# One step of a rational function's residual goes from VectorE to an adding DMA, with a new table of due times and another home for the ring of streamed weights

## Chip, cores, metric

The kernel runs on one core of one Trainium2 chip. The metric is the device time in microseconds of one execution. In what follows PE is TensorE, DVE is VectorE, ACT is ScalarE, POOL is GpSimd and SP is SyncE.

## What is computed

Three stages follow each other. Attention with a packed middle: `p` attends to `k`, `v`, and `q` attends to the result, for 8 batches, 8 heads, 576 positions and 32 packed rows. Then two feed-forward layers over the 4608 tokens of width 512, the first with a rational function, the second with h - tanh(h):

```
def _moe_ref(x, w_in, w_out, a, b):
    h = x @ w_in                      # 4608 x 512 @ 512 x 2048
    P = a[0] + a[1]*h + a[2]*h**2 + a[3]*h**3
    Q = 1.0 + abs(b[0])*abs(h) + abs(b[1])*h**2
    g = P / (Q + 1e-06)
    return g @ w_out                  # 2048 x 512
...
def _moe2_ref(x, w_in, w_out):
    h = x @ w_in
    return (h - tanh(h)) @ w_out
```

The weights arrive as float64 and are unpacked on the chip.

## The kernel before

Every product of the two layers is made from two reduced-precision parts, a high and a low one, so that each factor is split and three matmuls make one.

**Stage one** does attention and the first layer together. The tokens lie in 10 blocks (`XW`: 384, 512, 512, 512, 384, and the same again), and the 2048 hidden columns in 8 pairs of 128. A group g is one block with one pair: 80 groups, 48 of them with 2 x 512 = 1024 elements a partition and 32 with 768. For each group PE makes h (`l1`, line 643, two PSUM buffers), ACT and DVE make the polynomial P in tile `t` (lines 666, 681, 685), ACT makes |h| and a factor in `u` and `r` (670, 674), POOL or DVE multiplies them to the denominator in `m` (line 678, `front_q`), ACT turns it into a reciprocal `r` through Ln and Exp (690, 691), and `back` makes g in two parts for the second product (`l2`, line 656, with the high part 16 matmuls, with the low part 8):

- step 0 (698): the high part, gh = (t + a0) * r, rounded
- step 1 (700): m = (m + C0) * gh
- step 2 (704): m = (t + a0) - m, the residual
- step 3 (707): the low part, gl = m * r

The four are called b0 to b3 below; all four run on DVE. There are three `t`, two `m` and two `r`, with one more `m` and `r` in the middle of the stage, and one `gh` and one `gl` with one more each in the middle (`TEMPS`, `EXTRA`).

**The start** of stage one unpacks the weights: two `raw` tiles take turns, each filled by two transfers of 512 KB, shifted on DVE (342), scaled on ACT (350), joined on DVE (355), rounded on ACT (1215) and for the second weight split on DVE or POOL (1219).

**Stage two** (from about 780 us) is the second layer: tokens 0 to 511 with plain products (`l3`, line 770, and `l4`, lines 800 to 802), while combinations of the weights are prepared and stored to DRAM (833, 841, 850), then four blocks of 1024 tokens with seven products in place of eight, whose weights are streamed through a ring of four tiles (`ring_w`, used by line 977).

**The order** on every engine is set while the kernel is built, by the planner `Plan`: a list scheduler that knows a cost for each piece of work, picks what can start soonest on an engine, and among pieces that start within `SLACK` of that takes the one with the earliest due time. The due times come from the table `DUE`. Each engine then runs its list strictly in order, and waits on semaphores. What the costs say is the planner's; how long work takes is in the trace.

Of the kernel before, what the change touches and what calls it, by code (L numbers as in the profile page):

```python
# [7 lines left out]
F32 = mybir.dt.float32  # L8
# [8 lines left out]
LN_SHIFT = 63  # L17
LN2 = 0.6931471805599453


DUE = {"a_fq": 0.98, "a_b3": -15.108, "a_sl": -2.257, "a_sn": -4.221, "a_ss": -4.584, "a_xl": -7.444, "a_w4": -9.16, "a_w3": 15.573, "a_w2": -20.328, "G0": 4.368, "G1": 38.031, "A2": 4.694, "P_W": -6.643, "P_F": -18.924, "P_R": 2.448, "P_B": -19.51, "P_2": 3.012, "P_3": 12.129, "P_E": 10.733, "P_4": 17.691, "D_Y": -1.827, "b0": 22.093, "b1": -3.811, "b2": 2.98, "b3": -16.754, "l2h": 32.124, "l2l": 0.87, "f2": -30.567, "f3": -24.228, "fu": 3.235, "ft": 10.645, "fq": -31.176, "gH": -22.408, "gL": -35.399, "mx": -26.764, "ex": -60.969, "z": -8.638, "et": -7.472, "ta": 16.855, "av": -10.074, "y": 7.135, "bt": -42.785, "bd": -27.214, "si": -58.27, "sx": 25.69, "ss": 14.777, "se": -46.899, "sz": 13.095, "sn": 9.267, "so": 55.715, "sh": -7.194, "sl": -14.895, "w1": 20.251, "w2": -5.992, "w3": 17.226, "wh": -2.934, "wl": 18.386, "x": 7.951, "u2": 1.457, "u3": 13.153, "u4": 2.566, "u5": -25.368, "uu0": -1.378, "uu1": -1.334, "r0": -24.578, "dA": 37.158, "wd": -30.552, "d": 12.111}

SLACK = {"ALT": 0, "DVE": 7.5, "PE": 525.8, "ACT": 0, "POOL": 0, "SP": 734.4}

# [149 lines left out]
def packed_attention_moe_kernel(  # L174
# [81 lines left out]
    def pool_of(stack, name, bufs=1, **kw):  # L256
        return stack.enter_context(tc.tile_pool(name=name, bufs=bufs, reuse_waits="tile", **kw))
# [5 lines left out]

    tmp_p = pool_of(last, "tmp", side="right")

# [467 lines left out]
    oacc = {}  # L733
    yx = yt = stg = tw = None

# [6 lines left out]
    def x_load(b, k):  # L742
        t = yx.tile([128, 512], F32, tag="xr", name="xr", bufs=2)
        sp.dma_start(out=t, in_=x2d[:, k, NBLK * b:NBLK * b + NBLK])
        xr_t[b, k] = t
# [333 lines left out]
    def c_dve(n):  # L1079
        return 1.04 * n + 70  # L1080
# [156 lines left out]
    dma(("c",), 128 * 24, const_loads, due=-8)  # L1237
    add(("cabs",), "ACT", 100, lambda: act.activation(out=cabs, in_=cob, func=AF.Abs), [("c",)], -1)
    for b in range(B):
# [86 lines left out]


    add(("open t",), None, 0, close_start, [], 0, behind=[("bd", 0)])
    for g in range(total):
# [37 lines left out]
    def open_x():  # L1367
        nonlocal yx
        right.close()
        yx = pool_of(last, "yx", side="right")  # L1370
        x_buf(0)

    def open_y():
        nonlocal yt, stg, tw
        sx.close()
        stg = pool_of(ctx, "stg")
        ex = pool_of(ctx, "ex")
        yt = pool_of(ctx, "yt")
        tw = pool_of(ctx, "tw")
# [3 lines left out]
    sides = [("sl", NB - 1), ("g", B - 1, NP - 1), ("bd", 2 * B - 1), ("g", B - 1, NP - 2)]  # L1383
    add(("open x",), None, 0, open_x, sides, 0)
    add(("open y",), None, 0, open_y, [], 0,
# [11 lines left out]
    add(("open x", 1), None, 0, lambda: x_buf(1), [x for y in raw_user[-RAW:] for x in y], 0, behind=raw_next(("open x", 1)))  # L1397
    add(("open x", 2), None, 0, lambda: (x_buf(2), open_ring()), [("open x", 1), ("open x",)], 0)
    for b in range(3):
        for k in range(4):  # L1400
            e = d + (-12, 4, 20)[b] + 2 * k + O("x")
            n = 4 * b + k
            free = [("xl", *divmod(n - 2, 4))] if n >= 2 else []
            dma(("xr", b, k), 512 * 512, lambda b=b, k=k: x_load(b, k), [("open x",)] + reach(NBLK * b, NBLK) + free, e - 2 - 20 * (b > 0))
# [55 lines left out]
    for n, (kind, j) in enumerate(order):  # L1460
# [30 lines left out]
    for s in range(NS):  # L1491
# [82 lines left out]
        for n, i in enumerate(TWO):  # L1574
            for c in range(2):
                users = [("m4", s, i, f) for f in range(4 * c, 4 * c + 4)]
                have = [{1: ("pb", 4, j, 0), 2: ("pb", 4, j, 1), 3: ("pb", 4, j, 1)}.get(i, ("pd", 4, j)) for j in range(4 * c, 4 * c + 4)] if s == 0 else []
                if s == 0 and n < 2:
                    have += [("open x", 2), ("l3", n + 1, NF - 1)]
                stream(("wl4", s, n, c), 128 * 8192, lambda s=s, n=n, c=c: load_w4(s, n, c), have,  # L1580
# [33 lines left out]
        end = lambda i: ("m4", s, i, NJ2 - 1)  # L1614
        tmp_free = lambda x: [(x, s, NJ2 - 1)] if s else []
        for y in range(2):
# [70 lines left out]
```

## Time and profile before

| | |
|---|---|
| three timed runs | 1537.21, 1539.22, 1540.37 us, median 1539.22 |
| the profiled execution | 1536.59 us, its span 1534.7 us, so 1.9 us lie around the span |
| busy share of the span | PE 95%, DVE 85%, ACT 57%, POOL 9% |
| mean granted clock of PE | 0.985 |

The share of busy time is a mean over stages that differ: stage one and stage two are to be read apart. PE's matmuls are pipelined and the ends of their records are modelled, so a short wait can lie inside a busy PE.

### The profile page before, as it was taken

What the parts mean: (1) busy time and instruction counts of PE and PEld (TensorE: products, weight loads), DVE (VectorE), ACT (ScalarE), POOL (GpSimd) and SP (SyncE); (2) the same over time, 40 slices, a digit from 0 to 9 for tenths busy, and PEclk for the clock granted to TensorE, in tenths of its full rate; (3) what the DMA queues carried; (4) which work ended last, traced back from release to release, by engine and by line L of the source; (5) the groups of instructions that cost most, each with busy time, mean ns of one, the idle gap of its engine ahead of it and who ended that gap; (6) DMA issues with size and microseconds to landing.
All of it is one profiled execution on the core that took longest, in us unless ns stands there. A gap on an engine that the chain in (4) does not pass through costs nothing.

```text
span 1534.7 us, 21747 instructions
## 1 busy us (share of the span) xinstructions
PE 1462.3 (95%) x8448; PEld 1194.2 (78%) x8448; DVE 1307.3 (85%) x1690; ACT 878.3 (57%) x1216; POOL 135.2 (9%) x82
## 2 busy tenths in 40 slices
PE   5768999999999999999989999999999999999999
PEld 2657787878888878788877887777788878887787
DVE  5988999999999999999987885797789577957685
ACT  4776676677677767677766542453345333633353
POOL 0100011112111101222012110000000000000000
PEclk8888999999999999999999999999999999999999
DMA  7783314221332303132134696776656655665553
GB/s 255 269 267 129 125 56 143 86 103 59 136 119 76 132 31 132 60 131 83 42 109 187 193 279 250 280 290 221 246 204 241 222 182 206 231 218 192 205 192 137
DMA packets 74998, 257.86 MB, mean 168 GB/s; under 512 B 7184, under 2 KB 25744, under 8 KB 60048
## 3 DMA queue, kind: packets, MB, share of 16 engines
q1 hardware_dynamic: 74896, 256.47, 48.0%
q8 instruction: 67, 1.10, 0.3%
q14 instruction: 35, 0.29, 0.1%
HBM read 204.02 MB, written 52.43 MB: 167 GB/s over the span
## 4 chain that ended last, share of the span: by engine, by line
PE 68%; DVE 21%; ACT 5%; issue 3%; DMA 2%; POOL 1%; SPq 0%; DVEq 0%; ACTq 0%; POOLq 0%
PE acc L977 17%; PE acc L656 16%; PE h L977 12%; PE h L643 9%; PE h L770 9%; DVE yl L1020 2%; PE h L509 2%; DVE t L685 1%; DMA raw<-in_w_dram 1%; DVE gh L698 1%; DVE t L681 1%; DVE gl L707 1%; DVE m L704 1%; DVE m L700 1%; DVE slot L1012 1%
## 5 line engine op out<-in xcount | busy, mean ns | idle before, releaser
L643 PE MATMUL h<-ah,slot 128*128 128x320 f32 (+3 forms) x1024 | 215.8, 305 | 1.8 <-DVE slot L521 1.8
L656 PE MATMUL acc<-gh,slot 128*128 128x512 f32 (+1 forms) x800 | 177.6, 375 | 11.7 <-DVE slot L1219 11.3
L656 PEld LDWEIGHTS acc<-gh,slot 128*128 128x128 f32 x800 | 149.5, 195 | 36.0 <-DVE slot L1219 12.8
L643 PEld LDWEIGHTS h<-ah,slot 128*128 128x128 f32 x1024 | 171.4, 193 | 3.2 <-DVE slot L521 2.0
L656 PE MATMUL acc<-raw,slot 128*128 128x512 f32 (+1 forms) x720 | 164.6, 379 | 0.0
L643 PE MATMUL h<-al,slot 128*128 128x192 f32 (+3 forms) x512 | 151.4, 309 | 8.2 <-DVE t L685 4.1
L656 PEld LDWEIGHTS acc<-raw,slot 128*128 128x128 f32 x720 | 130.2, 188 | 31.9 <-issue 10.5
L1016 ACT ACTIVATE yh<-slot 128x512 fp32r<-128x512 f32 x140 | 87.0, 630 | 72.5 <-PE acc L977 30.6
L678 POOL TENSOR_TENSOR m<-u,r 128x1024 f32<-128x1024 f32 (+1 forms) x33 | 72.5, 2198 | 480.0 <-ACT r L674 372.7
L643 PEld LDWEIGHTS h<-al,slot 128*128 128x128 f32 x512 | 98.3, 192 | 18.0 <-DVE slot L521 2.9
L670 ACT ACTIVATE u<-h 128x1024 f32<-128x1024 f32 (+1 forms) x80 | 74.5, 931 | 60.7 <-PE h L643 60.4
L1020 DVE TENSOR_TENSOR yl<-slot,yh 128x512 fp32r<-128x512 f32 x140 | 95.5, 693 | 15.6 <-ACT yh L1016 14.8
L681 DVE TENSOR_TENSOR t<-t,h 128x1024 f32<-128x1024 f32 (+1 forms) x80 | 88.3, 1106 | 9.2 <-ACT t L666 8.9
L666 ACT ACTIVATE t<-h,coa 128x1024 f32<-128x1024 f32 (+1 forms) x80 | 89.3, 1119 | 10.9 <-PE h L643 6.5
L685 DVE SCALAR_TENSOR_TENSOR t<-t,coa,h 128x1024 f32<-128x1024 f32 (+1 forms) x80 | 93.3, 1166 | 1.9 <-ACT u L670 1.2
L656 PE MATMUL acc<-gl,slot 128*128 128x384 f32 (+1 forms) x400 | 92.3, 372 | 2.1 <-DVE gl L707 2.0
L690 ACT ACTIVATE r<-m,lnb 128x1024 f32<-128x1024 f32 (+1 forms) x60 | 63.6, 1060 | 53.7 <-POOL m L678 36.6
L770 PE MATMUL h<-xh,slot 128*128 128x512 f32 x256 | 83.9, 399 | 8.0 <-DVE t L779 6.4
L656 PEld LDWEIGHTS acc<-gl,slot 128*128 128x128 f32 x400 | 70.7, 188 | 20.3 <-issue 7.2
L1016 ACT ACTIVATE yh<-ex 128x512 fp32r<-128x512 f32 x84 | 52.6, 631 | 50.6 <-PE acc L977 25.5
L977 PE MATMUL acc<-yh,raw 128*128 128x512 f32 x256 | 78.9, 389 | 0.0
L999 ACT ACTIVATE t<-slot 128x512 f32<-128x512 f32 x45 | 28.5, 633 | 85.8 <-DVE slot L992 48.8
(196 smaller groups left out, 3237.4 us busy)
## 6 DMA issues: line engine op xcount, KB each, us to landing
raw<-in_w_dram SPq DMA_DIRECT2D x64, 512.0 KB, 4.5
w<-w1d SPq DMA_DIRECT2D x28, 1024.0 KB, 4.8
raw<-w4d SPq DMA_DIRECT2D x28, 1024.0 KB, 4.8
xh<-w4d SPq DMA_DIRECT2D x14, 1024.0 KB, 4.8
xl<-w4d SPq DMA_DIRECT2D x14, 1024.0 KB, 5.3
xh<-w3d SPq DMA_DIRECT2D x12, 1024.0 KB, 5.1
raw<-w3d SPq DMA_DIRECT2D x12, 1024.0 KB, 5.0
k<-in_kT_dram SPq DMA_DIRECT2D x16, 576.0 KB, 4.0
```

What stands on the lines that cost most here:

```text
L643: pe.matmul(out=ps[:, f, t], lhsT=x, rhs=y, start=(i == 0), stop=(i == len(seq) - 1))
L656: pe.matmul(out=acc_t[n][m][:, 0:XW[n]], lhsT=w2_slot[2 * p + f][:, o:o + 128], rhs=x[:, f, :], start=(p == 0 and part == 512 and f == 0), ...
L666: act.activation(out=t_t[g], in_=hv(g), func=AF.Identity, scale=a3, bias=a2)
L670: act.activation(out=u_t[g], in_=hv(g), func=AF.Abs)
L678: by.tensor_tensor(out=q_m[g], in0=u_t.pop(g), in1=r_t[g], op=ALU.mult)
L681: dve.tensor_tensor(out=t_t[g], in0=t_t[g], in1=hv(g), op=ALU.mult)
L685: dve.scalar_tensor_tensor(out=t, in0=t, scalar=a1, in1=hv(g), op0=ALU.add, op1=ALU.mult)
L690: act.activation(out=r, in_=q_m[g], func=AF.Ln, scale=2.0 ** -LN_SHIFT, bias=lnb[:, 0:1])
L770: pe.matmul(out=hy(b, f), lhsT=a, rhs=w, start=(j == 0), stop=(j == len(seq) - 1))
L977: pe.matmul(out=to, lhsT=a, rhs=b, start=(first and n == 0 and i in (1, 6, 7, 5)), stop=(last and n == len(seq) - 1), skip_group_check=True,)
L1016: act.activation(out=yh_t[s, i, f], in_=g_of(GSRC[i], f), func=AF.Copy)
L1020: by.tensor_tensor(out=yl_t[s, i, f], in0=g_of(GSRC[i], f), in1=yh_t[s, i, f].bitcast(F32), op=ALU.subtract)
```

## The change

Step 2 of `back` becomes a DMA that POOL issues: it adds the tile t onto the tile m. For that the sign of m is turned (Ln gets a negative scale, step 1 a negative C0, the absolute coefficients are negated by one more ACT instruction), and a0 goes into step 3, which is now a scalar_tensor_tensor on DVE only. The planner counts the DMA as 1100 ns of POOL and 4000 ns until it has landed.

The tables `DUE` and `SLACK` are replaced as a whole. The ring of streamed weights consists of the two `raw` tiles and two tiles `rg` of its own; before, its second half was the pair of x tiles. The x tiles are loaded through `made` and `rg`, and the small temporaries `tmp` open only after the last `l3`.

```
     def recip(g):
         r = r_t[g]
-        act.activation(out=r, in_=q_m[g], func=AF.Ln, scale=2.0 ** -LN_SHIFT, bias=lnb[:, 0:1])
+        act.activation(out=r, in_=q_m[g], func=AF.Ln, scale=-(2.0 ** -LN_SHIFT), bias=lnb[:, 0:1])
...
         if step == 1:
             dve.scalar_tensor_tensor(
-                out=u, in0=u, scalar=C0, in1=gh_t[g].bitcast(F32), op0=ALU.add, op1=ALU.mult
+                out=u, in0=u, scalar=-C0, in1=gh_t[g].bitcast(F32), op0=ALU.add, op1=ALU.mult
             )
         if step == 2:
-            dve.scalar_tensor_tensor(out=u, in0=t, scalar=a0, in1=u, op0=ALU.add, op1=ALU.subtract)
+            pool.dma_start(out=u, in_=t, accum_op=ALU.add)
         if step == 3:
             gl_t[g] = tmp(g, "gl")
-            by.tensor_tensor(out=gl_t[g], in0=u, in1=r, op=ALU.mult)
+            dve.scalar_tensor_tensor(out=gl_t[g], in0=u, scalar=a0, in1=r, op0=ALU.add, op1=ALU.mult)
...
+    LAND = 4000
...
-        add(("b2", g), "DVE", c_dve(HW) + 60, lambda g=g: back(g, 2), [("b1", g)], g + P_B + O("b2"), port=True)
-        add(("b3", g), ("POOL", "DVE"), (c_pool(HW), c_dve(HW)), lambda by, g=g: back(g, 3, by), [("b2", g)] + temp_old["gl", g], g + P_B + O("b3"), port=True)
+        add(("b2", g), "POOL", 1100, lambda g=g: back(g, 2), [("b1", g)], g + P_B + O("b2"), late=LAND, port=False)
+        add(("b3", g), "DVE", c_dve(HW) + 60, lambda g=g: back(g, 3), [("b2", g)] + temp_old["gl", g], g + P_B + O("b3"), port=True)
...
     def open_ring():
-        for b in (1, 2):
-            ring_w.extend(x.rearrange("p k t -> p (k t)") for x in x_bufs[b])
+        ring_w.extend(x.rearrange("p k t -> p (k t)") for x in x_bufs[1])
+        ring_w.extend(rg.tile([128, 2048], F32R, tag=f"rg{i}", name=f"rg{i}") for i in range(2))
...
-SLACK = {"ALT": 0, "DVE": 7.5, "PE": 525.8, "ACT": 0, "POOL": 0, "SP": 734.4}
+SLACK = {"ALT": 0, "DVE": 9.8, "PE": 104.4, "ACT": 0.0, "POOL": 2003.4, "SP": 0.0}
```

Line numbers of the changed kernel are 12 higher in `back` and around it: 678 becomes 690, 681 becomes 693, 685 becomes 697, 698 becomes 710, 700 becomes 712, the DMA is line 716, step 3 is line 719, and 1219 becomes 1237.

The first place is DVE in the middle of stage one, around two groups of 1024 elements (the seventh block). Before:

```order
L698 SCALAR_TENSOR_TENSOR raw<-t_229,coa,r_233 128x1024
L700 SCALAR_TENSOR_TENSOR m_235<-m_235,raw 128x1024
L681 TENSOR_TENSOR t_230<-t_230,h 128x1024
L521 TENSOR_TENSOR slot_86<-h,slot_86 128x512
L685 SCALAR_TENSOR_TENSOR t_230<-t_230,coa,h 128x1024
L521 TENSOR_TENSOR slot_87<-h,slot_87 128x512
L704 SCALAR_TENSOR_TENSOR m_235<-t_229,coa,m_235 128x1024
L707 TENSOR_TENSOR raw<-m_235,r_233 128x1024
L698 SCALAR_TENSOR_TENSOR gh_237<-t_230,coa,r_234 128x1024
L700 SCALAR_TENSOR_TENSOR m_236<-m_236,gh_237 128x1024
L704 SCALAR_TENSOR_TENSOR m_236<-t_230,coa,m_236 128x1024
```

The same place of the changed kernel (712 is step 1, 719 is step 3; `raw` is the additional low or high part):

```order
L712 SCALAR_TENSOR_TENSOR m_237<-m_237,raw 128x1024
L533 TENSOR_TENSOR slot_89<-h,slot_89 128x512
L710 SCALAR_TENSOR_TENSOR gh_239<-t_232,coa,r_236 128x1024
L712 SCALAR_TENSOR_TENSOR m_238<-m_238,gh_239 128x1024
L719 SCALAR_TENSOR_TENSOR raw<-m_237,coa,r_235 128x1024
L693 TENSOR_TENSOR t_233<-t_233,h 128x1024
L693 TENSOR_TENSOR t_231<-t_231,h 128x1024
L697 SCALAR_TENSOR_TENSOR t_233<-t_233,coa,h 128x1024
L719 SCALAR_TENSOR_TENSOR gl_240<-m_238,coa,r_236 128x1024
```

Step 2 is gone from DVE, and between step 1 and step 3 of one group there now stand three instructions for the first group (m_237) and four for the second (m_238).

The second place is DVE at the start, around the second unpacked tile of the first group. Before:

```order
L698 SCALAR_TENSOR_TENSOR gh_237<-t_229,coa,r_233 128x768
L521 TENSOR_TENSOR slot_87<-h,slot_87 128x512
L700 SCALAR_TENSOR_TENSOR m_235<-m_235,gh_237 128x768
L1219 TENSOR_TENSOR slot_68<-raw,slot_68 128x512
L704 SCALAR_TENSOR_TENSOR m_235<-t_229,coa,m_235 128x768
L681 TENSOR_TENSOR t_230<-t_230,h 128x768
L685 SCALAR_TENSOR_TENSOR t_230<-t_230,coa,h 128x768
L681 TENSOR_TENSOR t_231<-t_231,h 128x768
L707 TENSOR_TENSOR gl_238<-m_235,r_233 128x768
```

And in the changed kernel:

```order
L712 SCALAR_TENSOR_TENSOR m_237<-m_237,gh_239 128x768
L354 TENSOR_SCALAR raw<-raw 128x1024
L367 SCALAR_TENSOR_TENSOR raw<-raw 128x1024
L533 TENSOR_TENSOR slot_87<-h,slot_87 128x512
L1237 TENSOR_TENSOR slot_68<-raw,slot_68 128x512
L1237 TENSOR_TENSOR slot_69<-raw,slot_69 128x512
L354 TENSOR_SCALAR raw<-raw 128x1024
L693 TENSOR_TENSOR t_232<-t_232,h 128x768
L719 SCALAR_TENSOR_TENSOR gl_240<-m_237,coa,r_235 128x768
```

The unpacking of the next weights now stands between step 1 and step 3 of the first group.

The third place is POOL in the second half of stage one, where blocks of 768 give way to blocks of 1024. Before it had only the products for the denominator:

```order
L678 TENSOR_TENSOR m_236<-u_232,r_234 128x768
L678 TENSOR_TENSOR raw<-u_232,raw 128x768
L678 TENSOR_TENSOR m_236<-u_232,r_234 128x1024
L678 TENSOR_TENSOR raw<-u_232,raw 128x1024
L678 TENSOR_TENSOR m_235<-u_232,r_233 128x1024
```

In the changed kernel it issues the adding DMAs between them:

```order
L690 TENSOR_TENSOR m_237<-u_234,r_235 128x768
L716 DMA m_237<-t_231 128x768
L716 DMA m_238<-t_232 128x768
L716 DMA raw<-t_233 128x768
L716 DMA m_237<-t_231 128x1024
L716 DMA m_238<-t_232 128x1024
L690 TENSOR_TENSOR raw<-u_234,raw 128x1024
```

POOL has 80 DMAs to issue, 37 products (47 before) and one split of line 1237 (16 before). DVE has 80 step-2 instructions fewer, 10 products and 15 splits more.

## Rows read from the trace of the kernel before

**Rows 1.** The page's first part: span, busy time, share of the span, instructions.

```profile
span 1534.7 us, 21747 instructions
PE 1462.3 (95%) x8448; PEld 1194.2 (78%) x8448; DVE 1307.3 (85%) x1690; ACT 878.3 (57%) x1216; POOL 135.2 (9%) x82
```

**Rows 2.** Busy time by stretch: length, PE, PEld, DVE, ACT, POOL, clock, DMA share, GB/s.

```profile
0.00:57.00 57.00, 34.45 (x340) 23.58 (x341) 37.39 (x53) 33.60 (x51) 5.84 (x9) 0.85 0.77 262
57.00:153.00 96.00, 71.12 (x650) 58.17 (x649) 84.62 (x110) 63.52 (x97) 4.22 (x2) 0.89 0.61 210
153.00:767.00 614.00, 607.67 (x4220) 507.20 (x4219) 596.00 (x613) 435.88 (x516) 96.23 (x44) 1.00 0.27 95
767.00:844.00 77.00, 70.11 (x324) 59.66 (x323) 62.00 (x75) 48.86 (x70) 14.69 (x11) 0.96 0.41 147
844.00:1535.00 691.00, 678.90 (x2921) 545.58 (x2919) 527.31 (x842) 296.46 (x485) 14.21 (x17) 1.00 0.64 222
```

**Rows 3.** PE's longest wait, 153 to 767 us: sum, times, longest.

```profile
PE h L643 <- DVE t L685: 2.0, 4, 1.0
```

**Rows 4.** Chain of work from 153 to 767 us: shares by line, one long piece.

```profile
by line: PE acc L656 35.5%; PE h L643 21.0%; issue 3.8%; PE h L509 3.7%; DVE gh L698 3.2%; DVE t L685 3.2%; DVE t L681 2.7%; DVE m L700 2.4%; DVE m L704 2.3%; DVE gl L707 2.3%; DVE slot L521 1.4%; POOL m L678 1.2%; ACT slot L517 1.1%; PE h 
277.62 7.30 PE acc L656 x32
```

**Rows 5.** Chain of work from 57 to 136 us: shares by line, two pieces.

```profile
by line: DMA raw<-in_w_dram 14.7%; issue 9.7%; PE acc L656 6.3%; DVE slot L1219 5.5%; DVE gl L707 4.6%; DVE raw L355 4.5%; DVE slot L521 3.9%; DVE t L685 3.7%; DVE m L704 3.7%; ACT r L690 3.5%; DVE m L678 3.4%; DVE mx L440 3.4%; ACT t L666 
...
51.24 6.20 DMA raw<-in_w_dram
74.16 1.22 DVE raw L355
```

**Rows 6.** PE's longest waits, 767 to 844 and 844 to 1535 us.

```profile
PE h L770 <- DVE t L779: 6.4, 1, 6.4
...
PE h L977 <- DVE yl L1020: 3.4, 5, 2.0
```

**Rows 7.** DVE's groups by form: busy us, mean ns of one, idle before.

```profile
L704 DVE SCALAR_TENSOR_TENSOR m<-t,coa,m 128x1024 f32<-128x1024 f32 x34 | 44.9, 1320 | 0.2
...
L704 DVE SCALAR_TENSOR_TENSOR m<-t,coa,m 128x768 f32<-128x768 f32 x26 | 26.3, 1012 | 0.3
L698 DVE SCALAR_TENSOR_TENSOR gh<-t,coa,r 128x1024 fp32r<-128x1024 f32 x19 | 24.4, 1284 | 0.2 <-ACT r L691 0.2
...
L342 DVE TENSOR_SCALAR raw<-raw 128x1024 uint32<-128x1024 uint32 x31 | 23.2, 749 | 4.3 <-DMA raw<-in_w_dram 4.3
L700 DVE SCALAR_TENSOR_TENSOR m<-m,gh 128x1024 f32<-128x1024 f32 x19 | 23.1, 1217 | 0.3
L707 DVE TENSOR_TENSOR gl<-m,r 128x1024 fp32r<-128x1024 f32 x19 | 23.1, 1216 | 0.0
...
L1219 DVE TENSOR_TENSOR slot<-raw,slot 128x512 fp32r<-128x512 f32 x26 | 17.4, 686 | 2.0 <-ACT slot L1215 1.4
...
L678 DVE TENSOR_TENSOR m<-u,r 128x1024 f32<-128x1024 f32 x13 | 15.9, 1219 | 0.0
```

**Rows 8.** Busy time of line 704 alone, by stretch: length, DVE (instructions), clock, DMA.

```profile
57.00:153.00 96.00, 7.09 (x7) 0.89 0.61 210
153.00:767.00 614.00, 83.64 (x68) 1.00 0.27 95
```

**Rows 9.** DMA issues: KB each, median us from issue to landing.

```profile
raw<-in_w_dram SPq DMA_DIRECT2D x64, 512.0 KB, 4.5
w<-w1d SPq DMA_DIRECT2D x28, 1024.0 KB, 4.8
...
x2d<-q SPq DMA_DIRECT2D x12, 512.0 KB, 2.8
...
w1d<-slot SPq DMA_DIRECT2D x8, 512.0 KB, 6.6
```

**Rows 10.** POOL's product for the denominator, the largest group of POOL.

```profile
L678 POOL TENSOR_TENSOR m<-u,r 128x1024 f32<-128x1024 f32 (+1 forms) x33 | 72.5, 2198 | 480.0 <-ACT r L674 372.7
```

More of the change, by code (lines that the diff above doesn't have):

```diff
@@ L260, in packed_attention_moe_kernel @@
     right = ctx.enter_context(ExitStack())
-    tmp_p = pool_of(last, "tmp", side="right")
+    tw = pool_of(last, "tw", side="right")
     const = pool_of(ctx, "const")
@@ L733, in packed_attention_moe_kernel @@
     oacc = {}
-    yx = yt = stg = tw = None
+    yx = yt = stg = tmp_p = rg = None
+    sz = last.enter_context(ExitStack())
     def x_buf(b):
@@ L742, in x_load @@
     def x_load(b, k):
-        t = yx.tile([128, 512], F32, tag="xr", name="xr", bufs=2)
+        if b == 0:
+            if k == 0:
+                xr_t[-1] = tw.tile([128, 1024], F32, tag="made", name="made", bufs=1)
+            t = xr_t[-1][:, 512 * (k % 2):512 * (k % 2) + 512]
+        else:
+            t = ring_w[2].bitcast(F32)[:, 512 * k:512 * k + 512]
         sp.dma_start(out=t, in_=x2d[:, k, NBLK * b:NBLK * b + NBLK])
@@ L1237, in packed_attention_moe_kernel @@
     dma(("c",), 128 * 24, const_loads, due=-8)
-    add(("cabs",), "ACT", 100, lambda: act.activation(out=cabs, in_=cob, func=AF.Abs), [("c",)], -1)
+    add(("cabs",), "ACT", 200, lambda: (
+        act.activation(out=cabs, in_=cob, func=AF.Abs), act.activation(out=cabs, in_=cabs, func=AF.Copy, scale=-1.0)), [("c",)], -1)
     for b in range(B):
@@ L1369, in open_x @@
         right.close()
-        yx = pool_of(last, "yx", side="right")
+        yx = pool_of(sz, "yx", side="right")
         x_buf(0)
     def open_y():
-        nonlocal yt, stg, tw
+        nonlocal yt, stg, rg
         sx.close()
+        ex = pool_of(ctx, "ex")
+        rg = pool_of(ctx, "rg")
+        yt = pool_of(ctx, "yt")
         stg = pool_of(ctx, "stg")
-        ex = pool_of(ctx, "ex")
-        yt = pool_of(ctx, "yt")
-        tw = pool_of(ctx, "tw")
         for i in range(NF - NG):
@@ L1383, in packed_attention_moe_kernel, with open_z @@
     sides = [("sl", NB - 1), ("g", B - 1, NP - 1), ("bd", 2 * B - 1), ("g", B - 1, NP - 2)]
+    def open_z():
+        nonlocal tmp_p
+        sz.close()
+        tmp_p = pool_of(last, "tmp", side="right")
     add(("open x",), None, 0, open_x, sides, 0)
@@ L1397, in packed_attention_moe_kernel @@
     add(("open x", 1), None, 0, lambda: x_buf(1), [x for y in raw_user[-RAW:] for x in y], 0, behind=raw_next(("open x", 1)))
-    add(("open x", 2), None, 0, lambda: (x_buf(2), open_ring()), [("open x", 1), ("open x",)], 0)
+    add(("open x", 2), None, 0, lambda: (x_buf(2), open_ring()), [("open x", 1), ("open x",), ("open y",)], 0)
+    add(("open z",), None, 0, open_z, [], 0, behind=[("l3", 2, NF - 1)])
     for b in range(3):
@@ L1402, in packed_attention_moe_kernel @@
             n = 4 * b + k
-            free = [("xl", *divmod(n - 2, 4))] if n >= 2 else []
-            dma(("xr", b, k), 512 * 512, lambda b=b, k=k: x_load(b, k), [("open x",)] + reach(NBLK * b, NBLK) + free, e - 2 - 20 * (b > 0))
+            free = [("xl", 0, k - 2)] if b == 0 and k >= 2 else [("xl", 1, k)] if b == 2 else []
+            dma(("xr", b, k), 512 * 512, lambda b=b, k=k: x_load(b, k), [("open x", 2) if b else ("open x",)] + reach(NBLK * b, NBLK) + free, e - 2 - 20 * (b > 0))
             free = [[], [("open x", 1)], [("open x", 2), ("l3", 0, NF - 1)]][b]
@@ L1469, in packed_attention_moe_kernel @@
             need = [("ps", kind, j, 0), ("ps", kind, j, 1)] + (after("pl") if x == 0 else [("pm", kind, j, x - 1)])
+            if n == 0 and x == 0:
+                need += [("xl", 0, k) for k in range(4)]
             add(("pm", kind, j, x), EITHER, (c_low(256), c_dve(256)), lambda by, k=kind, j=j, x=x: prep_make(k, j, x, by),
@@ L1578, in packed_attention_moe_kernel @@
                 if s == 0 and n < 2:
-                    have += [("open x", 2), ("l3", n + 1, NF - 1)]
+                    have += [("open x", 2)] + ([("xl", b, k) for b in (1, 2) for k in range(4)] if n else [("l3", 1, NF - 1)])
                 stream(("wl4", s, n, c), 128 * 8192, lambda s=s, n=n, c=c: load_w4(s, n, c), have,
@@ L1614, in packed_attention_moe_kernel @@
         end = lambda i: ("m4", s, i, NJ2 - 1)
-        tmp_free = lambda x: [(x, s, NJ2 - 1)] if s else []
+        tmp_free = lambda x: [(x, s, NJ2 - 1)] if s else [("open z",)]
         for y in range(2):
```

6 lines of the change are left out of this document (5 added, 1 removed), and 8 rows, old and new, of the table DUE.

## The prediction

> **What bounds the kernel now.** I read the page's first part, then the stretches, then waits and chains stretch by stretch. The page says PE 95% and DVE 85% [rows 1]; the stretches say where. From 153 to 767 us, the body of stage one, both engines are full: PE 607.67 and DVE 596.00 of 614 us [rows 2]. The reader is to see there that two engines at 97% and more can both be the limit, and that relief of one is worth only what the other still waits. What PE still waits is little: it idles 6.3 us in 614, and its longest named wait sums to 2.0 us [rows 3]. Since short waits hide in modelled ends, I also took the start-to-start time of the recorded matmuls of lines 643 and 656 in this stretch, some 3000: 228 ns at 512 columns, as in the piece of 32 that takes 7.30 us [rows 4]. What exceeds the usual time of its width adds up to 20 us. So this stretch can give back between 0 and 20 us. That DVE lines make up a good part of its chain [rows 4] says the small waits are mostly for DVE.
>
> Before 153 us it is different. PE does 34.45 of 57 and 71.12 of 96 us at a clock of 0.85 and 0.89, while DVE works 84.62 of the 96 and the DMA engines 0.61 to 0.77 [rows 2]. The chain from 57 to 136 us runs through loads of `raw` (14.7%) and then DVE lines one after another, with ACT between them [rows 5]: the loop of two `raw` tiles, whose next load waits until DVE and ACT have emptied a tile. Here DVE time is worth time.
>
> After 844 us PE is busy 678.90 of 691 us and DVE has air [rows 2]; the one wait of size is 3.4 us for DVE's splits, and at the seam of the stages there is one of 6.4 us [rows 6].
>
> **What is removed.** Step 2, 80 instructions: 1.32 us for 1024 elements, 1.01 us for 768 [rows 7]. In the two stretches that matter that is 7.09 us (7) and 83.64 us (68) [rows 8].
>
> **What is added on DVE.** Ten more denominators, nine of them wide: 9 x 1.22 + 1.0 = 12 us, nearly all in the body. Step 3 as scalar_tensor_tensor: the nearest rows are step 0, which has the same form with a0 (1.284 us), and the present step 3 (1.216) [rows 7], so 0.07 us each, 4 us in the body; at least 0, since step 1 without a0 takes 1.217. Fifteen splits of line 1219 at 0.69 us [rows 7], 10 us, but the POOL splits that they replace stand at or behind the seam. Body: 596 - 84 + 12 + 4 = 528 of 614 us. DVE is left 86 us for 68 transfers, 1.26 us each.
>
> **What is added in waiting.** Step 3 now waits for a DMA, in order, so everything behind it on DVE waits too: the next group's polynomial, hence the PSUM buffer that `l1` needs, and the high part that `l2` needs. How long the DMA takes no row shows. It reads two tiles of 512 KB (384 in narrow blocks) and writes one. Lower bound: a store of 512 KB in the body lands in 2.8 us. Upper: 6.6 us for 512 KB between SBUF and DRAM, at the start [rows 9]. I take the row that moves as many bytes as the add reads, 1024 KB in 4.8 us [rows 9], plus 1 us for POOL to issue it (between 0 and the 2.2 us of a POOL product [rows 10]): 5.8 us in the body. For the start, where loads compete, I take 6.6 us in all.
>
> DMA: Bandwidth & Descriptors in the Trainium skill (section "Anatomy of one DMA — SWDGE (gpsimd) path") gives a plain GpSimd DMA as about 2.0 us plus bytes / 436e3; for 512 KB that is an estimate of 3.2 us, no run here shows it, and it would leave next to nothing of the stalls below.
>
> Against that stands the DVE work that the new order puts between step 1 and step 3. I summed the durations of the instructions between them for all 80 groups: half have more than 5.3 us, a quarter less than 3.9. In the excerpt of the body the two groups have 0.69 + 1.28 + 1.22 = 3.2 us and 1.28 + 1.21 + 1.21 + 1.27 = 5.0 us. The shortfall at 5.8 us is then 0.5 us for the middle group and 2 us for a short one. But the short ones come in pairs whose transfers overlap, so that one stall serves both. About 0.8 us each, against 1.26 us free: the stalls fit, with little to spare.
>
> The page SBUF — State Buffer of the Trainium skill (section "SBUF: two separate sides") has a rule against this change: while DVE runs a 2-port mode instruction, GpSimd can't write the descriptors of its DMAs, and they wait. The rows: only line 342 among the large DVE instructions runs 1024 elements in 0.749 us instead of 1.2 and more [rows 7], so only it looks like such a mode; it has 16 instructions before 153 us and 3 in the body. By that rule the start would lose at most 0.75 us for each of 8 transfers, 6 us, and the body nothing; the sum leaves it out.
>
> POOL itself has 37 products of 2.2 us and 80 issues of about 1 us, 160 us in 640: no bound. Buffers: t is held until the transfer lands and m and r until step 3, some 4.5 us longer. In the narrow blocks without the extra buffers (first and last eight groups) m lives about 0.95 (product) + 2 (Ln, Exp) + 1 + 1 + 5.8 + 1 = 12 us, and two of them serve two groups of PE work in 13 us. It fits, barely; this is the first thing to break if the DMA is slower.
>
> **The sum.**
> - Start: up to the low part of the second block of tokens DVE has 133 instructions instead of 147, 9.5 us less by their rows (7.1 of it step 2, the rest by order). Seven transfers stall it 0.6 us each (6.6 us against 5.3 us of work and the 12% of DVE's time that is idle there), so 4 back: -5.5 us. Bounds: -9.5 and +2.
> - Body: of 20 us that PE can regain, a third: -7. Bounds 0 and -20.
> - Seam: the last step 3 comes 4.8 us later than step 2 would have allowed (5.8 - 1.0); but the 6.4 us wait ends with ACT's and DVE's work for `l3`, much of which runs beside it: +2, bounds 0 and +4.8.
> - Stage two: the ring's second half can load before the last `l3`, no wait names it; splits prepared in other order: 0, bounds -3 and +3.
>
> From the profiled 1536.6 us that makes 1526; the median of the runs is 2.6 us above the profiled one, so **1529 us**. About 0.2%, 3 us, is what a measurement of this kernel tells from no change.
>
> **Rivals.**
> 1. *The transfer lands late and DVE becomes the bound again.* Same mechanism, price reversed. Stalls exceed DVE's free 1.26 us per transfer when the landing takes more than about 5.3 + 1.26 = 6.6 us with every transfer stalling alone, 7.9 us where pairs share. At 8 us: alone 68 x (2.7 - 1.26) = +98 us, shared +6; the 38 of 80 groups that overlap a neighbour put it near +30, and with the start's stalls 1555 to 1575 us. For it: the 6.6 us row [rows 9], the short gaps, the narrow blocks. Against it: the body's DMA share is only 0.27 [rows 2].
> 2. *The start loses.* The transfers move in the same DMA engines as the weights, which run at 262 GB/s and share 0.77 up to 57 us [rows 2]. Seven transfers read 7 x 768 KB; at that rate 20 us of transfer. If half delays `raw` loads, the loop on the chain [rows 5] slips 10 us, more than DVE gives: about 1540 to 1546 us.
> 3. *Nothing moves.* PE's body is full [rows 2, 3]; if its small waits are for ACT and PE's own results, relief of DVE shows as idle DVE, and the start is paced by loads: 1536 to 1542 us, the change of 84 us on DVE paid with no time at all.
> 4. *The new tables do harm elsewhere*, for instance at the seam, where POOL's splits have gone to DVE: included in the ranges.
>
> **How the numbers follow.** Forecast (1515 to 1535 us): 0.57. Late landing 0.20, the start 0.10, nothing 0.13. So faster 0.57, same 0.13, slower 0.30. The range for 8 in 10 goes from 1514, near the sum of the gains' bounds, to 1556, the near end of the late landing; the forecast's own range is 1515 to 1535 us.
>
> **What would show it.** Right: DVE in the body at 0.86 plus stalls, step 3 waiting for a DMA by under 1 us on average, landing near 5.8 us, PE's short waits shrunk, the block-two low part ready some 5 us earlier than before. Wrong: step 3's waits for DMA above 1.3 us a piece, PE idle growing from 6 us in the body to tens, `raw` loads taking longer than 4.5 us at the start, a longer wait than 6.4 us at the seam. The step most likely to fail is the landing time, which no row of before shows.

## The result and the profile after

The changed kernel takes 1557.5 us (median of 4 runs, 1557.1 to 1559.9) against 1539.4 us before (1537.2 to 1540.4, same chip): ratio 1.0123, 95% interval 1.0105 to 1.0140. It is slower by 1.2%, where 1529 us was forecast, and 1.5 us beyond the end of the range. Its profiled execution spans 1555.4 us.

The page's first part, its line on the queue of GpSimd's transfers (packets, MB, share of 16 engines), and the chain by engine answer to [rows 1]:

```profile
PE 1463.7 (94%) x8448; PEld 1196.1 (77%) x8448; DVE 1246.5 (80%) x1631; ACT 876.3 (56%) x1217; POOL 165.7 (11%) x141
...
q0 software_dynamic: 11520, 37.75, 12.8%
...
PE 61%; DVE 18%; DMA 7%; issue 4%; ACT 4%; POOL 1%; SPq 0%; DVEq 0%; ACTq 0%; POOLq 0%
```

DVE has lost 61 us of work and PE does what it did; a DMA now makes 7% of the chain, where the same line of the page of before has 2%:

```profile
PE 68%; DVE 21%; ACT 5%; issue 3%; DMA 2%; POOL 1%; SPq 0%; DVEq 0%; ACTq 0%; POOLq 0%
```

By stretch (columns as in [rows 2]):

```profile
57.00:153.00 96.00, 65.75 (x630) 51.33 (x630) 78.11 (x102) 63.15 (x95) 9.84 (x8) 0.84 0.74 236
153.00:767.00 614.00, 599.89 (x4174) 496.88 (x4173) 526.38 (x544) 426.27 (x508) 129.79 (x99) 1.00 0.54 146
767.00:844.00 77.00, 60.20 (x296) 53.45 (x297) 59.53 (x69) 47.42 (x62) 9.74 (x9) 0.93 0.49 132
844.00:1535.00 691.00, 685.09 (x2979) 556.95 (x2978) 539.75 (x857) 304.40 (x500) 13.10 (x17) 1.00 0.66 226
```

Against [rows 2] the body has DVE at 526 us (596 before), and PE has not gained by it: 599.9 against 607.7 us. Before 153 us and at the seam PE does 5 and 10 us less. The DMA share in the body has doubled, 0.54 against 0.27. What DVE waits for (sum, times, longest), from the list of its waits over the span:

```profile
DVE gl L719 <- DMA m<-t: 29.3, 13, 5.6
...
DVE raw L719 <- DMA m<-t: 13.7, 8, 2.8
...
DVE raw L719 <- DMA raw<-t: 10.5, 5, 2.9
...
DVE gl L719 <- DMA raw<-t: 4.8, 2, 2.7
```

Line 719 is step 3. It waits 28 times, 58.3 us in all, for the transfer of step 2 (under the name `raw` the same tile lies in an extra buffer). The mean over 80 groups is 0.73 us, but 22 of the waits are above 1.2 us and make 53.4 us of the sum. PE in turn waits for step 3, over the span (2.0 us in 3 waits before):

```profile
PE acc L668 <- DVE gl L719: 13.3, 8, 3.5
```

The times from issue to landing on the page, for the loads of `raw` and the adds of wide and narrow groups:

```profile
raw<-in_w_dram SPq DMA_DIRECT2D x64, 512.0 KB, 5.7
...
m<-t POOLq DMA_DIRECT2D x34, 512.0 KB, 4.6
...
m<-t POOLq DMA_DIRECT2D x26, 384.0 KB, 4.9
```

These times run from the start of the issue, so the 0.87 to 0.89 us that POOL takes to issue one are in them. From the end of step 1 to the landing it is 5.6 us in the mean of groups 9 to 71 and 5.0 at the median, by the records of the trace. The spread is wide: 3.8 to 10.4 us from issue to landing, 18 of the 80 above 6 us. Those 18 stand beside other transfers, whose packets keep the 16 engines busy for 17 to 72% of the time to the landing (median 46%); the 39 adds with less than 10% of such company land in 3.8 to 5.5 us. The loads of `raw` beside them went from 4.5 [rows 9] to 5.7 us. The chain from 54 to 173 us (start, length, what) shows where single transfers take longer:

```profile
61.30 0.96 DVE m L712
62.56 7.55 DMA m<-t
70.14 1.02 DVE gl L719
...
90.53 8.22 DMA m<-t
98.77 1.03 DVE gl L719
...
156.61 9.22 DMA m<-t
165.93 1.03 DVE gl L719
167.01 2.10 PE acc L668 x8
```

Here the transfer stands on the path itself, from step 1 (L712) to step 3 and on to `l2` (L668). Transfers of the last groups of stage one stand on it too, in the chain from 767 to 832 us:

```profile
768.63 0.97 DVE m L712
...
770.00 5.54 DMA m<-t
...
802.39 7.37 DMA m<-t
...
809.85 1.02 DVE gl L719
```

To place the difference I took the recorded starts of three matmuls from each trace: the first `l2` matmul of block 1, that of block 9, and the first of stage two's layer (line 977 before, 995 after), and the start of its last one. All records of these lines are there. Stretches in us from each kernel's profiled execution, with the medians of the kernels that follow. The stretches of one execution add up to that execution and not to the median; the two lie up to 8 us apart (e14: 1581.7 and 1573.4), so a difference of 2 or 3 us in one stretch is near what single executions tell:

| kernel | median | to block 1 | block 1 to 9 | block 9 to stage two | stage two |
|---|---|---|---|---|---|
| before | 1539.4 | 161.4 | 584.0 | 233.3 | 552.0 |
| after | 1557.5 | 173.2 | 590.8 | 245.3 | 541.6 |
| e1 transfer alone | 1584.2 | 166.6 | 618.6 | 243.6 | 548.9 |
| e2 tables alone | 1591.0 | 172.1 | 627.6 | 238.2 | 547.8 |
| e3 ring alone | 1533.1 | 164.3 | 583.8 | 232.4 | 549.0 |
| e4 tables and ring | 1589.9 | 169.7 | 628.0 | 239.6 | 547.4 |
| e13 tables and transfer | 1566.8 | 167.9 | 593.5 | 247.2 | 547.0 |
| e5 step 2 left out | 1525.9 | 161.4 | 578.5 | 240.0 | 541.6 |
| e6 step 2 on DVE, same order | 1567.8 | 163.1 | 611.0 | 242.5 | 541.5 |
| e7 copy not awaited | 1528.3 | 160.7 | 578.6 | 239.9 | 541.7 |
| e18 two copies not awaited | 1537.5 | 161.8 | 580.8 | 244.5 | 541.5 |
| e8 first nine groups without | 1545.9 | 159.7 | 592.5 | 244.3 | 541.6 |
| e9 step 3 reads t | 1540.7 | 164.9 | 582.4 | 247.1 | 541.5 |
| e17 step 3 reads r | 1537.3 | 161.9 | 583.4 | 243.0 | 541.5 |
| e10 half transfer | 1538.6 | 165.9 | 581.6 | 241.9 | 541.6 |
| e11 14 groups on DVE | 1552.9 | 167.9 | 585.6 | 246.2 | 541.6 |
| e12 step 2 on GpSimd | 1593.1 | 167.7 | 632.0 | 245.1 | 541.5 |

From before to after: +11.8 at the start, +6.8 in the body, +12.0 at the seam, -10.4 in stage two, +20.2 in all (18.1 between the medians).

### The profile page after: what moved, and what is told of

It reads as the page before. It is cut to its first block, busy times and chain, and to the rows that moved or that the text cites. A ratio compares the mean times of both kernels' runs of the same rounds, so it can differ in the third digit from the quotient of the medians.

```text
span 1555.4 us, 21764 instructions
## 1 busy us (share of the span) xinstructions
PE 1463.7 (94%) x8448; PEld 1196.1 (77%) x8448; DVE 1246.5 (80%) x1631; ACT 876.3 (56%) x1217; POOL 165.7 (11%) x141
## 4 chain that ended last, share of the span: by engine, by line
PE 61%; DVE 18%; DMA 7%; issue 4%; ACT 4%; POOL 1%; SPq 0%; DVEq 0%; ACTq 0%; POOLq 0%
PE acc L668 17%; PE acc L995 15%; PE h L995 10%; PE h L655 8%; PE h L788 6%; DMA m<-t 5%; DVE yl L1038 3%; PE h L521 2%; DVE slot L1030 1%; DVE slot L945 1%; DMA raw<-t 1%; POOL m L690 1%; DVE gh L710 1%; DVE gl L719 1%; PE h L444 1%
## 5 line engine op out<-in xcount | busy, mean ns | idle before, releaser
L668 PE MATMUL acc<-gh,slot 128*128 128x512 f32 (+1 forms) x800 | 176.4, 373 | 5.7 <-DVE slot L1237 5.4
L668 PEld LDWEIGHTS acc<-gh,slot 128*128 128x128 f32 x800 | 148.0, 193 | 32.6 <-issue 6.7
L668 PE MATMUL acc<-raw,slot 128*128 128x512 f32 (+1 forms) x720 | 165.9, 381 | 0.9 <-DVE raw L719 0.8
L668 PEld LDWEIGHTS acc<-raw,slot 128*128 128x128 f32 x720 | 129.6, 188 | 37.5 <-issue 12.7
L668 PE MATMUL acc<-gl,slot 128*128 128x384 f32 (+1 forms) x400 | 92.7, 374 | 13.3 <-DVE gl L719 13.3
L716 POOL DMA_DIRECT2D m<-t x60 | 53.3, 888 | 373.8 <-DVE m L712 363.0
L668 PEld LDWEIGHTS acc<-gl,slot 128*128 128x128 f32 x400 | 71.3, 190 | 28.2 <-DVE gl L719 16.4
L995 PE MATMUL h<-slot,rg 128*128 128x512 f32 x336 | 80.0, 393 | 1.2 <-DVE slot L1010 0.2
```

What stands on the lines that cost most here:

```text
L668: pe.matmul(out=acc_t[n][m][:, 0:XW[n]], lhsT=w2_slot[2 * p + f][:, o:o + 128], rhs=x[:, f, :], start=(p == 0 and part == 512 and f == 0), ...
L716: pool.dma_start(out=u, in_=t, accum_op=ALU.add)
L995: pe.matmul(out=to, lhsT=a, rhs=b, start=(first and n == 0 and i in (1, 6, 7, 5)), stop=(last and n == len(seq) - 1), skip_group_check=True,)
```

## The experiments

**The three parts apart.** Each of e1 to e4 and e13 is the kernel before with only some hunks of the diff; the planner writes the order for each.

```diff
 e1:  recip, back, ("b2", g), ("b3", g), cabs as after;  DUE, SLACK, ring as before
 e2:  DUE, SLACK as after;                               the rest as before
 e3:  open_ring, x_load, open_y, open_z, tw as after;    the rest as before
 e4:  e2 and e3;   e13: e1 and e2
```

> The kernel before with step 2 as the adding transfer and nothing else: old tables (DUE, SLACK), old ring; the planner writes the order anew. Theory A (the transfer costs the time: it lands late beside the loads of the start and at the seam): 1550 to 1570 us, its transfers of the first 160 us landing in more than 6.6 us of issue and flight, PE late by some 12 us at block 1. Theory B (the new tables cost it): 1525 to 1540 us, the gain that was forecast. Theory C (the ring's new place costs it): as B.

> The kernel before with the new DUE and SLACK alone; step 2 stays on the vector engine, the ring as before. Theory A: 1535 to 1545 us, and the stretch after 844 us some 10 us shorter if the tables' order of stage two is what gave back 10 us in the changed kernel. Theory B: 1550 us or more, with block 1 late by 10 us or more. Theory C: 1539 within 3 us.

> The kernel before with the ring of streamed weights and the x tiles at their new places alone. Theories A and B: 1539 within 5 us, the start untouched (nothing before 760 us depends on it but where tiles lie). Theory C: 1550 us or more, lost behind 760 us.

> The changed kernel without the transfer: new tables and new ring, step 2 (and step 3 as before) on the vector engine. Theory A: below the changed kernel by 12 to 25 us, so 1530 to 1545 us. Theories B and C: 1550 to 1560 us, as the changed kernel.

> The changed kernel without the ring's move (old ring, old x tiles): new tables and transfer alone. If the ring is worth the same as alone (5.6 us faster): 1560 to 1566 us. If the ring costs time in this company: 1552 us or less. If the 6 to 10 us of stage two come from ring and transfer together: 1562 to 1570 us, with 547 us or more of the stretch of line m's matmuls.

Measured: 1584.2, 1591.0, 1533.1, 1589.9 and 1566.8 us. None of the theories A, B and C, which put the cost on one part, holds. The transfer in the old order costs 46 us, and the new tables without the transfer 52 us; e4 against e2 shows that the ring doesn't mend that. Together they cost 29 us (e13), and with the ring 18. The tables and the transfer belong to each other: between block 1 and block 9 the transfer alone loses 35 us and the tables alone 44, both together 10. e1 lies above all its ranges, e2 fits theory B (1550 or more, block 1 late by 10 us or more), e4 lies above all its ranges, and e3, 5.6 us faster, is just outside the 5 us that A and B allowed. The ring costs nothing. Alone it is faster than the kernel before, ratio 0.9956, interval 0.9939 to 0.9972, and in the company of the others it brings 9 us by the medians (e13 against after; e13's three executions range from 1562 to 1570 us). e13 fits its third case, 1562 to 1570 us with 547.0 us in stage two. **Of the versions that compute the whole sum, e3 is the one that beats both kernels.**

**What the transfer costs in the changed kernel's own order.** The planner's entries stay, so the order stays; only what step 2 or step 3 issues is changed.

```diff
 step 2:  pool.dma_start(out=u, in_=t, accum_op=ALU.add)
 e5:      (nothing)
 e6:      dve.tensor_tensor(out=u, in0=u, in1=t, op=ALU.add)
 e7:      pool.dma_start(out=spare[g][:, :, 0:XW[g // NP]], in_=t)
 e8:      the transfer if g >= 9, else nothing
```

> The changed kernel in its own order, with step 2 left out: nothing is added to u, so the low part of gl is not the right sum, and step 3 waits for no transfer. Theory A (waiting for the landing, and the transfer's traffic, cost the time): 1530 us or less, the start some 4 to 6 us earlier, the 53 us of step 3's waits gone, PE 20 us shorter to the end of stage one. Theory B (the order that the new tables make costs it, with or without a transfer): 1545 us or more, block 1 still 8 us or more later than in the kernel before. What is saved here is all that any faster transfer could bring.

> The changed kernel's order with step 2 as a plain add on the vector engine, at the place where the transfer was issued. Theory A: the same as the changed kernel or faster, 1545 to 1560 us, since 1.2 us of DVE replaces a wait of about as much. Theory B, and the premise of the forecast that DVE time is worth time in the body: 1575 to 1595 us, as the new tables with step 2 on DVE (1590 us).

> The changed kernel's order; step 2 is issued as a plain transfer of t to a spare place in device memory that nobody reads, so the add is left out, step 3 waits for no transfer, and only t stays held until the transfer has read it. Theory A with the wait as the cost: within 3 us of the kernel with step 2 left out. Theory A with the traffic as the cost: within 8 us of the changed kernel, the loads of raw at the start at 5 us or more. Theory B: within 3 us of the changed kernel, as with step 2 left out.

> The changed kernel's order with step 2 left out for the first nine groups alone (up to the second block of tokens; the add is missing there). Theory A with the start as the place: 1545 to 1550 us, block 1 some 5 to 8 us earlier than in the changed kernel and the gain kept to the end. Theory A with the body as the place: block 1 earlier, the gain lost again, 1552 us or more. Theory B: 1555 to 1559 us, block 1 unmoved.

Measured: 1525.9, 1567.8, 1528.3 and 1545.9 us. Theory A holds in e5, e7 and, for the start, e8; B falls: with no transfer the new order gives 1526 us, 3 us under the forecast. That this is so near is luck: by stretch e5 has 0, -5.5, +6.7 and -10.4 us against before, where the sum had -5.5, -7, +2 and 0. So the transfer costs 32 us in this order, and 12 of them come with the first nine groups. The windows of e5, columns as above:

```profile
57.00:153.00 96.00, 71.61 (x685) 58.60 (x686) 83.75 (x108) 67.52 (x101) 3.93 (x3) 0.88 0.62 218
153.00:767.00 614.00, 607.45 (x4226) 507.78 (x4224) 541.37 (x554) 434.21 (x516) 75.17 (x34) 1.00 0.27 93
```

PE gets through 685 matmuls between 57 and 153 us instead of 630, at a granted clock of 0.88 instead of 0.84 (a mean over time at 2.4 and at 1.2 GHz; before each fall PE had stood waiting for part of the time). Both come back with step 2 gone. The clock can have at most a small part in it: e17 below gets through the same 685 at a granted clock of 0.86. e6 is 10 us slower than the changed kernel, against theory A's range and short of theory B's: in this order the transfer is better than the instruction that it replaces. But not everywhere: to block 1 the add on DVE is 10 us quicker, in the body 20 us slower. Against e5, e6 also tells what DVE's relief is worth in this order: 32.5 us in the body (611.0 to 578.5) and 1.7 us at the start.

**Wait or traffic.** All transfers run; step 3 is given another operand, so that only its wait goes. e18 loads the DMA engines without anyone waiting but ACT for `t`.

```diff
 step 3:  dve.scalar_tensor_tensor(out=gl_t[g], in0=u, scalar=a0, in1=r, ...)
 e9:      in0=t
 e17:     in0=r
 e18:     step 2 as in e7, twice, to two spare places
```

> The changed kernel with all its transfers as they are; only step 3 reads t in place of u, so the low part is not the right sum and step 3 waits for no landing. The traffic, the issues on POOL and the holding of t and m until the transfer has landed all remain. Theory A (DVE standing in front of step 3 is the cost): 1524 to 1533 us, within 5 us of the kernel with step 2 left out. Theory D (the adding transfer costs by its traffic or by the buffers that it holds, which the plain copy showed only in part): 1540 us or more.

> The changed kernel with all its transfers; step 3 reads r in place of u, so the low part is not the right sum, step 3 waits for no landing, and t is held until the transfer has read it and no longer. If the 15 us left with step 3 reading t were its longer hold on t: 1528 to 1533 us. If they are the transfer's load or its hold on m: 1538 to 1543 us.

> The changed kernel's order, step 2 issued as two plain copies of t to spare places that nobody reads; m is not held, t until both have read it. The copies load the DMA engines about as long as the adding transfer, some 26% of the body against 27%. If the load is what costs: 1536 to 1542 us. If it is the hold on m: 1527 to 1532 us, as with one copy.

Measured: 1540.7, 1537.3 and 1537.5 us. e9 meets theory D's bound of 1540, e17 misses its second range by 0.7 us, and e18 lies in the first of its two. In e9 step 3 also holds `t` longer, which e17 does not; the two differ by 3 us. So of the 32 us the wait of step 3 is 20 (after against e17) and the rest 11 (e17 against e5, by the medians; their profiled executions, from which the stretches come, lie 8.7 us apart). One copy that nobody awaits costs 2 us, two cost 12, and two load the engines about as the add does, as the lines of the DMA queues between 153 and 767 us say (packets, MB, share of 16 engines), first e7:

```profile
q0 software_dynamic: 9008, 32.51, 13.2%
```

then e18:

```profile
q0 software_dynamic: 18016, 65.02, 26.7%
```

and e17, with the adding transfer:

```profile
q0 software_dynamic: 9792, 33.03, 28.0%
```

The load with the hold on `t` can thus explain the 11 us, and the hold on `m` isn't needed for it. The match is in the total alone: the copies go to device memory, and against e5 e18 loses 2.3 us in the body and 4.5 at the seam, e17 4.9 and 3.0. How the 11 split between load and hold on `t` stays open: ACT waits 20.3 us for the transfers before it can write `t` in e17, 6.2 us in e18. At the start this load costs nothing: e17 reaches block 1 at 161.9 us, as e5, although its loads of `raw` between 40 and 153 us take 5.9 us instead of 5.0. So of the 11.8 us that the start loses to the transfer (173.2 against 161.4) 11.3 are the wait.

**Less landing, or the long waits taken out.**

```diff
 e10:  pool.dma_start(out=u[:, 0:1, :], in_=t[:, 0:1, :], accum_op=ALU.add)
 e11:  step 2 as in e6 for g in [1, 3, 8, 13, 14, 26, 37, 38, 41, 45, 46, 48, 56, 64]
```

> The changed kernel with the transfer cut to the first of the two planes of 512 (or 384) columns; the other half is not added. It moves half the bytes. Theory A with a landing that is mostly a fixed time: landing 3.5 to 4.2 us against 4.6, so about 0.7 us less for each stall, 1545 to 1553 us. Theory A with a landing that goes by bytes: landing 2.5 us, hardly a stall left, 1528 to 1536 us. Theory D: half of the 32 us that the transfer costs comes back, 1540 us, whatever the landing.

> The changed kernel's order; the 14 groups whose step 3 stood over 1.2 us in front of a transfer (34 us together) do step 2 on the vector engine, the other 66 by transfer. Theory A with few long stalls as the cost: DVE gains 34 - 14 x 1.15 = 18 us, of which two thirds reach the end (32 of 46 us did when all were taken away): about 1545 us, between 1540 and 1549. A rival: the stalls move to the next groups, since the later ones are now early: 1552 us or more.

Measured: 1538.6 and 1552.9 us. Half the bytes land in 3.2 us against 4.6; a straight line through the two medians gives an estimate of some 1.8 us that is fixed and 0.7 us for each 128 KB. The waits of step 3 fall from 58.3 to 25.2 us and the time by 19 us. That fits both waiting and load, which are halved together here; it does not tell them apart. e11 gained 4.6 us where 12 were expected. The choice of groups was incomplete: a semaphore entry just ahead of step 3 hid eight more waits above 1.2 us. Counted rightly the changed kernel has 22 of them, 53.4 us. In e11 three sums in DVE's waits for transfers remain, 19.5, 6.8 and 3.3 us: 28.7 us of waits were bought with 15 us of adds. The net 13 us brought 4.6 us by the medians (the profiled execution, from which the waits are read, took 1547.9 us). The waits of the 14 groups made 34.0 us, so 5.3 us of new waits stand at other groups: the rival, that the stalls move on, has part of it.

**GpSimd instead of the DMA.**

```diff
 e12:  step 2:  pool.tensor_tensor(out=u, in0=u, in1=t, op=ALU.add)
```

> The changed kernel's order; step 2 is a plain add on GpSimd at the place of the issue, 2.4 us for 1024 elements by its product of the same shape, no transfer. Theory A: 2.4 us plus a signal is under the 5 us of vector work that the order has between steps 1 and 3, so no stall: 1526 to 1535 us, faster than the kernel before, if both engines keep their pace. A rival: GpSimd and the vector engine slow each other when they read the same memory, so that vector instructions beside the 80 adds take 1.5 us in place of 1.2 or the adds 4 us or more: 1550 us or more.

Measured: 1593.1 us, the rival. Three groups of DVE's instructions in e12 (busy us, mean ns of one | idle before):

```profile
L710 DVE SCALAR_TENSOR_TENSOR gh<-t,coa,r 128x1024 fp32r<-128x1024 f32 x19 | 35.2, 1853 | 7.1 <-ACT r L703 4.3 <-PE acc L668 2.7
...
L697 DVE SCALAR_TENSOR_TENSOR t<-t,coa,h 128x1024 f32<-128x1024 f32 x48 | 60.9, 1269 | 0.4
...
L690 DVE TENSOR_TENSOR m<-u,r 128x1024 f32<-128x1024 f32 x18 | 29.9, 1661 | 2.7 <-ACT r L686 2.7
```

and the same in the changed kernel:

```profile
L710 DVE SCALAR_TENSOR_TENSOR gh<-t,coa,r 128x1024 fp32r<-128x1024 f32 x19 | 24.3, 1279 | 3.0 <-ACT r L703 2.9
...
L697 DVE SCALAR_TENSOR_TENSOR t<-t,coa,h 128x1024 f32<-128x1024 f32 x48 | 61.0, 1272 | 0.3
...
L690 DVE TENSOR_TENSOR m<-u,r 128x1024 f32<-128x1024 f32 x18 | 22.0, 1220 | 0.8 <-ACT r L686 0.6
```

Step 3 waits for the add only once, 1.9 us, so waiting for it is not the cost here. Instructions with two operands in SBUF go from 1279 to 1853 and from 1220 to 1661 ns; line 697, which takes `h` from PSUM, stays at 1270. The Trainium skill has this rule in SBUF — State Buffer, section "SBUF: two separate sides": DVE with two SBUF inputs and a GpSimd operation that reads SBUF shut each other out for a whole instruction, and DVE in a 2-port mode and GpSimd likewise. The trace agrees for the instructions shown. Line 354 (342 before), with one operand, goes from 692 to 875 ns; it would have to be such a mode, which no run shows.

**An order planned for the true landing.**

```diff
 e14:  LAND = 4600      e15:  LAND = 5500
 e16:  late=(7000 if g < 9 else 6000 if g >= 72 else 4600)
```

> The changed kernel with LAND = 4600 in place of 4000; the planner writes the order anew. Theory P (the order reckons the landing too short): 1540 to 1552 us, the stalls of step 3 from 58 us to 35 us or less. Rival (the order's slack is set by the tables, and a new order is as likely worse): 1557 or more, the stalls 45 us or more.

> The changed kernel with LAND = 5500. Theory P: 1535 to 1550 us, stalls of step 3 under 25 us. Rival: 1557 us or more; fewer stalls at step 3, but other work late in their place (l2 waiting for the low part, l1 for its PSUM buffer).

> The changed kernel with the landing planned by place: 7000 for the first nine groups, 6000 for the last eight, 4600 for the rest. Theory P: the best of the three, 1535 to 1548 us, block 1 some 5 us earlier. Rival: no better than the changed kernel, 1555 us or more, since where nothing else is ready the wait is the same wherever it is planned.

Measured: 1573.4, 1563.0 and 1576.3 us, with step 3 waiting 50.2, 32.7 and 34.5 us for transfers. The rival: the waits named at step 3 shrink by up to 26 us and the kernel is still slower, by 5 to 19 us, most of it in the body (615.7, 597.5 and 608.0 us from block 1 to 9). With the same tables an order planned for a later landing loses elsewhere what step 3 wins. So the planner's reckoning of the landing is not the cause by itself, at least not with these tables.

## Why the prediction was wrong, by its own steps

**DVE's relief: right in its direction, forecast 13 us too large.** 528 us was worked out for the body and 526.4 stands there, but by luck: the late kernel has 544 instructions in that window, where 613 - 68 + 10 = 555 were reckoned. e5, with 554, has 541.4 us. The sum took single durations (84 us) from a busy time in which records overlap: the 596 us are 636 as a sum of durations. That relief is worth time is shown in the new order alone (e6 against e5). Without step 2 the body takes 578.5 us against 584.0 before, 5.5 us less where the sum had 7; since the order changed with it, no run shows that these are the same 5.5 us.

**Landing in the body: right in the mean, wrong in its spread.** 5.8 us with the issue was assumed for every group; from the end of step 1 the mean is 5.6 us, but single landings take 3.8 to 8.8 us there from the issue. At the start 6.6 us was assumed; the three transfers on the chain took 7.6, 8.2 and 9.2 us to land, the issue included, and the nine from 4.3 to 10.4. The estimate from the Trainium skill's DMA: Bandwidth & Descriptors (section "Anatomy of one DMA — SWDGE (gpsimd) path"), 3.2 us, is near the plain copy of e7 (3.7 us for 512 KB) and 1.4 us below the adding one. The rule of SBUF — State Buffer on locked-out descriptors, weighed in the prediction, doesn't explain the long landings: behind the issues of groups 2 and 4 line 354 (342 before) ran for 0.69 us and they landed in 4.3 and 4.5 us, while groups 7 and 8, with none of it, took 9.2 and 10.4. POOL's issues took 0.85 to 1.32 us up to 160 us, half a microsecond of delay at most.

**The step that failed: "About 0.8 us each, against 1.26 us free: the stalls fit, with little to spare."** The mean was right, 58.3 / 80 = 0.73 us, by luck, since 52 groups do not wait for their transfer at all. One landing time for every group, and a mean stall set against DVE's mean free time, were wrong. The stalls are not 80 small ones: 22 of 1.4 to 5.6 us carry 53 of 58 us. By the trace of the changed kernel they stand where a long landing meets little work: their transfers land in 6.3 us at the median, those of the other 58 groups in 4.4, and DVE has 3.8 us of work between steps 1 and 3 instead of 5.2. An estimate by arithmetic alone: 21 of the 58 us would be left if no landing had taken more than 4.6 us. The prediction spoke against late landing with the body's mean DMA share of 0.27; other transfers come in bursts, and beside them single adds land late. That the company causes the late landing is read from the trace; no run took it away. While DVE stands there, its free time elsewhere is of no use to the `l2` or `l1` that waits for what is queued behind. Removing the wait alone gives back 20 us by the medians, and in the profiled executions 11.3 at the start, 7.4 in the body, 2.3 at the seam. The start's term (-5.5, with 0.6 us for each of seven transfers) fails by the same step: its nine groups have four waits of 1.4 to 4.4 us, 11.4 us together. The relief itself brought nothing there (161.4 us without step 2, as before), so the term's gain of 9.5 us, which rested on the order as well, did not come. Two of the prediction's own signs of being right came true all the same, a wait under 1 us on average and a landing near 5.8 us: both are means.

**A term that was missing: the transfers' load.** The sum had it as a rival for the start alone. There it costs nothing (e17), so rival 2 falls as it was put. Behind the start it costs 5 us in the body and 3 at the seam (e17 against e5), with the hold on `t` in it; at which groups was not taken apart.

**Seam and stage two.** +2 and 0 were forecast, +12.0 and -10.4 measured. Of the seam, 6.7 us is there without any transfer (240.0 against 233.3), 3.0 is the load and 2.3 the wait: what goes with the new order and ring in the main, which the sum did not price. Of stage two's -10.4, 5.4 is the ring's new place (e13 against after: 547.0 and 541.6), of which 4.3 lie in the last five sixths of stage two, told in the last section; in other company the ring is worth 3.0 (e3) and 0.4 us (e4 against e2). The other 5.0 came with the new order, 4.2 with the tables alone (e2), and was not taken apart further. That is the prediction's rival 4 on both sides, and its bounds of +4.8 and of 3 us either way were too narrow.

**Rival 1** named the mechanism, and its time (1555 to 1575) holds the result, but not its condition: it was to begin at a landing of 6.6 us, and it was there at 5.6 in the mean. Its chance of 0.20 was too low for that reason: by the step that failed, the wait was taken to be free up to DVE's mean reserve.

## What to carry to other kernels

A wait in an in-order queue is priced place by place, as landing less the work that stands between, with the landing's spread and what else the DMA engines do at that place, and not as a mean against the engine's mean idle time. Before a transfer is made faster or moved, leave it out in the same order and then let its reader read something else: two runs gave the ceiling (1526 us) and the split of the loss (20 waiting, 11 load). And parts that were fitted to each other must be taken apart with care: the tables alone lose 52 us, the transfer alone 46, while the third part by itself was a gain of 5.6.

## What the runs showed of the hardware

**Where a streamed weight lies changes the pace of its matmul.** The ring alone makes the kernel 5.6 us faster, and 4.5 us of that can be the pace of these matmuls, as the last lines of this paragraph say. From 1180 to 1500 us PE runs, before

```profile
1180.00:1500.00 320.00, 318.81 (x1374) 256.55 (x1374) 240.11 (x379) 131.79 (x220) 0.00 (x0) 1.00 0.60 209
```

and in e3

```profile
1180.00:1500.00 320.00, 317.92 (x1387) 259.02 (x1386) 242.91 (x384) 132.30 (x223) 0.00 (x0) 1.00 0.60 210
```

13 more matmuls at the same clock. By the recorded starts, a matmul of 512 columns that reads a ring tile in the old place of `xh` or `xl` takes about 233 ns to the next start, some half of them; one that reads `raw`, or the new `rg`, takes about 227. The last five sixths of stage two take 456.1 to 456.2 us with the old ring (before, e2, e13) and 451.6 to 451.8 with the new (e3, e4, after). The tiles have the same shape; what in the place makes the difference no run shows.

**An adding transfer costs the DMA engines twice a copy to device memory**: between 153 and 767 us the changed kernel has

```profile
q0 software_dynamic: 9392, 31.95, 27.1%
```

against 13.2% for 32.51 MB in e7. A wide one lands in 4.6 us against 3.7, and takes POOL 0.89 us to issue against 0.62.

**GpSimd slows DVE where DVE reads two operands from SBUF**, by 36 to 45% in the two such groups of e12 shown above; the same form with one operand in PSUM keeps its 1270 ns. Line 354, with one operand in SBUF, is slower too (692 to 875 ns), so two operands are not the only case.
